# Attention and two MLPs on one core: the subtractions of 1 and the roundings beside the attention go to GpSimd, with a new order

## The chip, the core and the metric

The kernel runs on one core of a Trainium2 chip. The engines of the core work side by side, each through its own queue of instructions in order: TensorE (PE: matmul products, with PEld for its weight loads), VectorE (DVE), ScalarE (ACT), GpSimd (POOL) and SyncE (SP), which here only issues transfers. GpSimd issues some transfers too. The metric is the device time of one execution in microseconds (us), as the median of several runs.

## The reference

Attention over 4 sequences with 8 heads of 576 x 64, in which each row keeps only the scores that lie within tau of its largest, and then two MLPs one after the other over the 2304 tokens.

```python
batch, n_heads, seq, head_dim = (4, 8, 576, 64)        # n_tokens, d_model, d_ff = (2304, 512, 2048)
scores = scale * np.matmul(q, k.transpose(0, 1, 3, 2))
thresh = np.max(scores, axis=-1, keepdims=True) - tau
scores = np.where(scores >= thresh, scores, -1000000000.0)
attn = np.exp(scores - np.max(scores, axis=-1, keepdims=True))
attn = attn / (np.sum(attn, axis=-1, keepdims=True) + 1e-09)
x = np.matmul(attn, v)                                  # to (2304, 512)
h = x @ w_in
g = np.where(h > 0.0, h, 1.0 * (np.exp(np.minimum(h, 0.0)) - 1.0))
x = g @ w_out                                           # first MLP
h = x @ w_in2
out = np.maximum(0.01 * h, h) @ w_out2                  # second MLP
```

The weights come as 64-bit floats; the kernel reads their two 32-bit halves.

## The kernel before, in words

The d_ff dimension is cut into 16 slices f of 128. The work has four stages on TensorE:

1. Attention, and beside it the first MLP's slices f = 0 to 7 for seven blocks of 256 tokens (0 to 1791), whose partial y goes to the scratch tensor `yp`.
2. The same slices for the last 512 tokens, in 512 columns.
3. The first MLP's slices f = 8 to 15 for all tokens, in blocks of 512, added to `yp`.
4. The second MLP, all slices.

**Products in three passes.** An fp32 product is made of three faster ones: each operand is split into a rounded high part and the rest (x into `xh` and `xl`, g into `gh` and `gl`, a weight into `wih` or `woh` and a low part that is named `wil`, `wol` or plain `w` with a number). Every h or y step of one f is 12 products, 4 k or m of 3 passes. Only the first block of 256 tokens runs with whole fp32 operands (`whole` in the code: `h<-x,w` and `y<-gh,w` with 4 products in a step).

**Attention.** A pair of heads with 4 or 5 units of 64 rows is a group's piece; there are 32 pieces. Per unit: scores `s` on TensorE; `ss` on VectorE (scaled, with the row's extreme); threshold `thr`; two steps on ScalarE (`ss`, then the exponential `e` with its sum); the reciprocal `su` on VectorE; `e` times it on GpSimd. Then e is transposed: the first four pieces on TensorE (`y<-ident,e`, then copies into `p`), the other 28 in 32x32 squares on VectorE (`t<-e`) and by 16 copies of 32 partitions from `t` to `p`, issued by SP and by GpSimd. Then `v<-p,v` on TensorE and a copy into `x`.

**One f step beside the attention.** TensorE writes h for slice f into one half of a PSUM bank (`hbank`, two halves in turn). ScalarE takes the exponential into `g`, one of VectorE and GpSimd subtracts 1 (`km`), VectorE takes the min and max with h, which frees the half, one engine rounds g to `gh` (`kg`), VectorE or GpSimd makes `gl = g - gh` (`kgl`), and two steps later TensorE uses both for y. When a block is done, two copies bring y from PSUM to the staging tile `ysa`, and a transfer takes that to `yp`.

**What sets the order.** The program is a list of operations, each with the engines that may do it (the letters in `KN`: A, D, P), a cost and a due time worked out from numbers in `KN`. `Order.run` lays them out greedily on the engines by these costs, and the instructions are written in that order. On the chip every engine then goes through its own list in order and waits where data is not ready.

**End of the attention.** `close_attn` gives the attention's tiles back and opens the tiles of the later stages in their place. It stands behind `end_a`, which before depends on every operation listed so far. `ysa` lies in the pool `ac`, which is given back there.

## Time and profile before

| | us |
|---|---|
| median of 3 runs (lowest, highest) | 1043.79 (1040.55, 1047.26) |
| the profiled execution | 1044.41 |
| its span in the profile | 1042.6 |
| PE busy in the span | 1005.2 (96%) |
| DVE busy | 569.2 (55%) |
| ACT busy | 507.0 (49%) |
| POOL busy | 392.0 (38%) |

The span is the time from the first to the last instruction; the profiled execution took 1.81 us more than that. "Busy" is the time in which at least one instruction ran on the engine. The stages are very unlike each other, so that the shares of the whole span say little about any one of them; the mean granted clock of TensorE over the span is 0.992 of full speed.

### The profile page before, as it was taken

To read this page: it belongs to the slowest core of one execution; us is meant where nothing else is said; L and a number is where in the kernel's file an instruction comes from. 1 tells how busy PE (TensorE), PEld (TensorE's weight loads), DVE (VectorE), ACT (ScalarE), POOL (GpSimd) and SP (SyncE) were. 2 spreads that over 40 slices of the span, in tenths; PEclk is the share of its full clock that TensorE was granted. 3 is DMA by queue.
4 is the path that set the end of the run, shared out by engine and by line. 5 is a ranking of instruction groups with operands and counts; after the bars stand their busy time and mean duration, and the time that the engine had idled before them with its cause. 6 is when DMAs were issued, how large, how long until landed. Compare 5 with 4: busy or idle time off the path is not lost.

```text
span 1042.6 us, 17014 instructions
## 1 busy us (share of the span) xinstructions
PE 1005.2 (96%) x6228; PEld 795.3 (76%) x6228; DVE 569.2 (55%) x1146; ACT 507.0 (49%) x1009; POOL 392.0 (38%) x542
## 2 busy tenths in 40 slices
PE   6869999999999998999999999999999999999998
PEld 3446676677676776888888889888888888888898
DVE  6888778787887856767786457442211311311121
ACT  6967767677777753555455235432222311322221
POOL 5678977567577752444443013440000000000000
PEclk8999999999999999999999999999999999999999
DMA  6676876766778653353443103320100100000010
GB/s 213 209 216 175 221 195 192 227 188 196 201 209 240 192 150 119 102 182 101 143 141 101 61 21 86 118 61 0 41 1 1 41 1 1 22 19 1 1 41 21
DMA packets 47554, 115.93 MB, mean 111 GB/s; under 512 B 9776, under 2 KB 14384, under 8 KB 47472
## 3 DMA queue, kind: packets, MB, share of 16 engines
q1 hardware_dynamic: 42960, 104.36, 33.4%
q0 software_dynamic: 4512, 10.50, 3.7%
q8 instruction: 49, 0.80, 0.3%
q14 instruction: 33, 0.27, 0.1%
HBM read 67.63 MB, written 9.44 MB: 74 GB/s over the span
## 4 chain that ended last, share of the span: by engine, by line
PE 90%; DVE 3%; DMA 2%; ACT 2%; issue 1%; POOL 0%; SPq 0%; ACTq 0%; DVEq 0%; POOLq 0%
PE y L678 37%; PE h L624 22%; PE hb L624 15%; PE v L582 7%; PE s L475 7%; PE y L674 1%; DMA p<-t 1%; PE h L621 1%; DVE w L346 1%; DMA taut<-in_tau_dram 1%; DVE ss L479 1%; DMA wraw<-in_w1i_dram 1%; PE y L513 0%; DVE xl L307 0%; ACT e L493 0%
## 5 line engine op out<-in xcount | busy, mean ns | idle before, releaser
L307 DVE TENSOR_TENSOR gl<-g,gh 128x512 fp32r<-128x512 f32 (+1 forms) x150 | 101.1, 675 | 284.4 <-ACT g L656 265.0
L678 PE MATMUL y<-gh,woh 128*128 128x512 f32 (+1 forms) x704 | 245.5, 349 | 2.1 <-ACT ysa L318 1.4
L678 PE MATMUL y<-gl,woh 128*128 128x512 f32 (+1 forms) x704 | 242.8, 345 | 0.0
L624 PE MATMUL h<-xh,wih 128*128 128x256 f32 (+1 forms) x448 | 153.1, 342 | 9.2 <-ACT g L639 5.1
L678 PEld LDWEIGHTS y<-gh,woh 128*128 128x128 f32 x704 | 132.5, 188 | 29.1 <-issue 8.8
L624 PE MATMUL h<-xl,wih 128*128 128x256 f32 (+1 forms) x448 | 148.6, 332 | 0.7 <-DVE xl L307 0.6
L678 PEld LDWEIGHTS y<-gl,woh 128*128 128x128 f32 x704 | 132.7, 188 | 16.1
L498 POOL TENSOR_SCALAR e<-e,su 128x576 f32<-128x576 f32 x144 | 113.9, 801 | 32.2 <-DVE su L496 30.9
L678 PE MATMUL y<-gh,w 128*128 128x256 f32 (+1 forms) x384 | 124.9, 325 | 0.0
L490 ACT ACTIVATE ss<-ss,thr 128x576 f32<-128x576 f32 x144 | 104.6, 767 | 34.5 <-DVE thr L485 34.4
L479 DVE TENSOR_SCALAR_CACHE_REDUCE ss<-s,scl 128x576 f32<-128x576 f32 x144 | 113.8, 798 | 10.9 <-PE s L475 10.7
L678 PE MATMUL y<-gh,wol 128*128 128x512 f32 (+1 forms) x320 | 117.7, 368 | 0.0
L518 DVE STREAM_TRANSPOSE t<-e 128x640 f32<-128x640 f32 x128 | 101.2, 823 | 17.9 <-POOL e L498 12.5
L493 ACT ACTIVATE e<-ss,taun 128x577 f32<-128x577 f32 x144 | 110.5, 768 | 0.3
L624 PEld LDWEIGHTS h<-xh,wih 128*128 128x128 f32 x448 | 84.2, 188 | 33.2 <-issue 8.8
L475 PE MATMUL s<-in 64*64 64x288 f32 x1152 | 91.3, 428 | 7.8 <-DVE ss L479 7.8
L624 PE MATMUL hb<-xh,wih 128*128 128x512 f32 (+1 forms) x256 | 94.6, 369 | 0.0
L624 PE MATMUL hb<-xl,wih 128*128 128x512 f32 (+1 forms) x256 | 94.5, 369 | 0.0
L582 PE MATMUL v<-p,v 128*64 128x320 f32 (+1 forms) x640 | 87.1, 417 | 5.3 <-DVE p L319 2.3
L624 PEld LDWEIGHTS h<-xl,wih 128*128 128x128 f32 x448 | 84.3, 188 | 10.0 <-DVE xl L307 1.8
L624 PE MATMUL h<-xh,w 128*128 128x256 f32 (+1 forms) x288 | 89.3, 310 | 0.0
L654 ACT ACTIVATE gh<-h 128x512 fp32r<-128x512 f32 (+1 forms) x40 | 22.2, 555 | 132.4 <-PE h L624 132.4
(207 smaller groups left out, 1591.4 us busy)
## 6 DMA issues: line engine op xcount, KB each, us to landing
p<-t SPq DMA_DIRECT2D x128, 100.0 KB, 2.8
p<-t SPq DMA_DIRECT2D x144, 80.0 KB, 3.3
v<-in_kqv_dram SPq DMA_DIRECT2D x32, 320.0 KB, 3.8
in<-in_kqv_dram SPq DMA_DIRECT2D x16, 608.0 KB, 4.2
in<-in_kqv_dram SPq DMA_DIRECT2D x16, 544.0 KB, 4.0
wraw<-in_w1i_dram SPq DMA_DIRECT2D x16, 512.0 KB, 4.3
wraw<-in_w1o_dram SPq DMA_DIRECT2D x16, 512.0 KB, 3.6
wraw<-in_w2i_dram SPq DMA_DIRECT2D x16, 512.0 KB, 3.5
```

Of the source, the lines that this page charges most:

```text
L307: return pick(who, D=(dve(n), lambda: nc.vector.tensor_tensor(**args()), PORT), P=(pool_tt(n), lambda: nc.gpsimd.tensor_tensor(**args())))
L346: ob = op((DVE, dve(512), lambda: nc.vector.scalar_tensor_tensor(out=b().bitcast(U32), in0=top(), scalar=0x80000000, in1=b().bitcast(U32), ...
L475: nc.tensor.matmul(s[z]()[64 * h:64 * h + 64, i, 0:HALF], q()[r, at:at + 64], k()[r, h], start=True, stop=True)
L479: om = [op((DVE, dve(S) + 160, lambda z=z: nc.vector.tensor_scalar(out=ss[z]()[:, 0:S].rearrange("p (j c) -> p j c", j=2), in0=s[z]()[:, : ...
L490: o = op((ACT, act(S) + 95, lambda z=z: nc.scalar.activation(out=ss[z]()[:, 0:S], in_=ss[z]()[:, 0:S], func=AF.Prelu, bias=thr()[:, z:z + ...
L493: oe.append(op((ACT, act(S) + 190, lambda z=z: nc.scalar.activation(out=e[z]()[:, 0:S + 1], in_=ss[z]()[:, 0:S + 1], func=AF.Exp, bias=tau ...
L498: on = [op(pick(KN["kn"], P=(pool_ts(S) + 90, lambda z=z: nc.gpsimd.tensor_scalar(out=e[z]()[:, 0:S], in0=e[z]()[:, 0:S], scalar1=su()[:, ...
L518: turned.append(op((DVE, dve(SX) + 70, lambda z=z, cols=cols: nc.vector.transpose(out=blocks(tg).rearrange("p d c q -> p c d q")[:, :, :, ...
L582: nc.tensor.matmul(ps()[64 * h:64 * h + 64, 0:64 * n], v()[:, h, c, :], blocks(pg)[:, 2 * h:2 * h + 2, c], start=(c == 0), stop=(c == 4))
L624: nc.tensor.matmul(hp(), w_()[:, cs], x_()[:, 0:tb], start=(k == 0 and z == 0), stop=(k == KC - 1 and z == 2))
L654: o1 = op((ACT, actp(tb), lambda: nc.scalar.activation(out=gh()[:, cs], in_=hp(), func=AF.Prelu, alpha=0.01)), [o], [hg, gh], vt)
L678: nc.tensor.matmul(ysl(yg, m), w_()[:, cs], g_()[:, 0:tb], start=(first and z == 0 and share == 0), stop=(last and z == 2 and end))
```

## The change: what it does, and the diff

- The subtraction of 1 (`km`) may only be done by GpSimd; before, VectorE or GpSimd. This holds beside the attention and in the later stages of the first MLP.
- The rounding of g to `gh` beside the attention (`kg`) goes from ScalarE to GpSimd. After the attention it stays on ScalarE.
- The low parts of weights that are made after the attention (`ko`) go from GpSimd to VectorE. The second layer's `gl` (`kgl1`) may be made by GpSimd too.
- Of the 16 copies from `t` to `p` GpSimd issues four instead of five (`NG`), SP twelve instead of eleven.
- `ysa` is taken from the pool `const`, which lasts to the end, and `end_a` depends on what was listed before the last block's copies out of y, not on these and their transfer.
- The other numbers of `KN` (due times) are new, so that the order of nearly all instructions changes. `GROUPS`, `FIRST`, `PT` and `whole` are written in another way with the same values; the new third alternative for `kt` is not chosen.

```diff
-NG = 5
+NG = 4
-SPI = 720
+SPI = 700
...
-    pad=18, stay=1957.74, late=1.3, margin=0, look=0.00236881, warm=2, tu=2525.65, lead=19496.6, wv0=975.379,
-    wv1=-2861.01, early=3673.33, boff=26347.2, bdt=5788.03, yoff=6965.78, coff=5895.83, wb=140.292, w2a=-207.297,
+    pad=18, stay=7714.83, late=1.3, margin=0, look=0.00215667, warm=2, tu=2531.97, lead=19496.6, wv0=975.379,
+    wv1=-2667.23, early=3947.77, boff=37932.2, bdt=5788.03, yoff=12797.6, coff=5895.83, wb=-716.662, w2a=-228.739,
...
-    o3=-792.8, o4=-3200.93, o5=4767.88, o6=-24.0285, mo=-2162.59, ka='P', kl='PA', kh='PA', ko='P', kt='D', kx='A',
-    kxl='DP', km='DP', kg='A', kgl='DP', kgl1='D', kd='P', kc='AD', kn='P', kv='AD')
+    o3=-1828.01, o4=-608.895, o5=4748.06, o6=-26.8192, mo=-4085.5, ka='P', kl='PA', kh='PA', ko='D', kt='D', kx='A',
+    kxl='DP', km='P', kg='P', kgl='DP', kgl1='DP', kd='P', kc='AD', kn='P', kv='AD')
...
-    ysx = []
+    ysx = [const.tile([128, KC, TA], F32, name="ysa")]
...
-    ysx.append(ac.tile([128, KC, TA], F32, name="ysa"))
...
     def evac_a(t0, tb, ybank, ysl, last, xc, vt):
+        since[0] = len(od.ops)
         ys = ys_r.new()
...
-    end_a = op((HOST, 0, lambda: close_attn()), list(od.ops), [], 0)
+    end_a = op((HOST, 0, lambda: close_attn()), od.ops[:since[0]], [], 0)
```

How the order changes is shown at three places.

The first is TensorE between the last `v` of the four pieces that TensorE transposes and the first `v` of a piece whose squares are moved by copies. `h<-x,w` and `y<-gh,w` are whole fp32 products of the first block. Before, the rows from just behind the one `v` to the other:

```order
L621 MATMUL h<-x,w_143 128x256
L621 MATMUL h<-x,w_230 128x256
L475 MATMUL s<-in 64x288 x8
L621 MATMUL h<-x,w_230 128x256 x3
L475 MATMUL s<-in 64x288 x12
L621 MATMUL h<-x,w_324 128x256 x4
L674 MATMUL y<-gh,w_196 128x256 x4
L621 MATMUL h<-x,w_439 128x256 x2
L582 MATMUL v<-p_86,v 64x320 x10
```

There are 11 products of h and 4 of y. With the change, the same place, behind one more row of 8 score products:

```order
L625 MATMUL h<-x,w_143 128x256
L625 MATMUL h<-x,w_236 128x256 x4
L477 MATMUL s<-in 64x288 x8
L625 MATMUL h<-x,w_324 128x256 x2
L477 MATMUL s<-in 64x288 x4
L625 MATMUL h<-x,w_324 128x256 x2
L625 MATMUL h<-x,w_435 128x256 x3
L477 MATMUL s<-in 64x288 x8
L625 MATMUL h<-x,w_435 128x256
L678 MATMUL y<-gh,w_179 128x256 x4
L678 MATMUL y<-gh,w_287 128x256 x2
L586 MATMUL v<-p_86,v 64x320 x10
```

There are 13 products of h and 6 of y, and the score products stand in smaller rows between them.

The second place is GpSimd's list in the middle of the attention stage, around the start of the fifth block of 256 tokens. Before (`e` is the multiplication by the reciprocal sum, `g` the subtraction of 1, DMA the issue of copies from `t` to `p`):

```order
L498 TENSOR_SCALAR e_91<-e_91,su 128x576
L568 DMA p_87<-t_89 32x640 x5
L498 TENSOR_SCALAR e_92<-e_92,su 128x576
L498 TENSOR_SCALAR e_93<-e_93,su 128x576
L643 TENSOR_SCALAR g<-g 128x256
L498 TENSOR_SCALAR e_90<-e_90,su 128x576
L498 TENSOR_SCALAR e_91<-e_91,su 128x576
L643 TENSOR_SCALAR g<-g 128x256
L308 TENSOR_TENSOR gl<-g,gh 128x256
L643 TENSOR_SCALAR g<-g 128x256
```

With the change, the list at the same block:

```order
L572 DMA p_87<-t_89 32x640
L572 DMA p_87<-t_89 32x800 x2
L572 DMA p_87<-t_89 32x640
L502 TENSOR_SCALAR e_92<-e_92,su 128x576
L502 TENSOR_SCALAR e_93<-e_93,su 128x576
L647 TENSOR_SCALAR g<-g 128x256 x2
L502 TENSOR_SCALAR e_90<-e_90,su 128x576
L502 TENSOR_SCALAR e_91<-e_91,su 128x576
L314 TENSOR_SCALAR gh<-g 128x256
L311 TENSOR_TENSOR gl<-g,gh 128x256
L647 TENSOR_SCALAR g<-g 128x256
```

Two subtractions stand in a row behind four issues and two steps of `e`, and the rounding `gh` is in the list.

The third place is SP at the end of the attention: the last piece's copies, the last block's transfer to `yp`, and the first loads of raw weights for the later slices. Before:

```order
L568 DMA p_87<-t_89 32x640
L568 DMA p_87<-t_89 32x800 x4
L731 DMA yp_dram<-ysa 512x1x256
L326 DMA wraw<-in_w1i_dram 128x1024
L326 DMA wraw<-in_w1o_dram 128x1024
```

With the change:

```order
L572 DMA p_87<-t_89 32x640
L572 DMA p_87<-t_89 32x800 x2
L329 DMA wraw<-in_w1i_dram 128x1024
L737 DMA yp_dram<-ysa 512x1x256
L329 DMA wraw<-in_w1o_dram 128x1024
```

The first weight load has moved ahead of the transfer to `yp`. On ScalarE the first `xh` of the last 512 tokens still stands behind the last step of the attention stage, in both orders.

## Rows read from the trace of the kernel before

**Rows 1.** Windows by stage: start:end, length, busy us and instructions by engine, clock, DMA share, GB/s.

```profile
0.00:20.00 20.00, 13.10 (x83) 5.72 (x83) 11.86 (x33) 11.31 (x20) 9.97 (x21) 0.83 0.62 221
20.00:55.00 35.00, 28.34 (x257) 16.89 (x259) 29.72 (x70) 32.91 (x65) 24.89 (x32) 0.95 0.67 209
55.00:80.00 25.00, 17.48 (x103) 10.96 (x101) 22.31 (x43) 16.64 (x32) 18.80 (x25) 0.87 0.66 196
...
100.00:385.00 285.00, 276.22 (x2468) 201.23 (x2467) 223.06 (x555) 208.99 (x464) 204.13 (x329) 1.00 0.72 202
385.00:405.00 20.00, 16.52 (x114) 12.46 (x113) 7.66 (x15) 4.39 (x10) 4.63 (x8) 1.00 0.53 153
405.00:700.00 295.00, 294.59 (x1389) 247.42 (x1388) 196.62 (x295) 137.42 (x231) 112.49 (x106) 1.00 0.32 102
```

**Rows 2.** Timeline of PE, 60 to 77 us: start, us, instruction, idle before and releaser.

```profile
64.79 0.72 PE L475 MATMUL s<-in 64*64 64x288 f32 x8 [2.41 <-DVE ss L479]
66.92 1.24 PE L475 MATMUL s<-in 64*64 64x288 f32 x8 [1.42 <-DVE ss L479]
...
70.99 1.89 PE L674 MATMUL y<-gh,w 128*128 128x256 f32 x8
...
76.56 0.95 PE L582 MATMUL v<-p,v 128*64 128x320 f32 x3 [2.20 <-DMA p<-t]
```

**Rows 3.** The chain that ended last, around the end of the attention: start, us, what.

```profile
389.91 5.26 PE y L678 x45
...
397.32 3.58 DMA yp_dram<-ysa
...
401.39 0.64 ACT xh L313
```

**Rows 4.** Timeline of PE, 395 to 403 us.

```profile
395.94 0.39 PE L678 MATMUL y<-gh,woh 128*128 128x256 f32 x1 [0.78 <-DVE ysa L319]
...
396.50 3.12 PE L582 MATMUL v<-p,v 128*64 128x320 f32 x20
402.07 0.50 PE L624 MATMUL h<-xh,wih 128*128 128x512 f32 x1 [2.46 <-ACT xh L313]
402.80 0.50 PE L624 MATMUL h<-xl,wih 128*128 128x512 f32 x1 [0.22 <-DVE xl L307]
```

**Rows 5.** Timeline of PE, inside one group of h products at 382 us.

```profile
382.75 0.38 PE L624 MATMUL h<-xh,wih 128*128 128x256 f32 x1 [0.53 <-ACT g L639]
```

**Rows 6.** DVE by line and shape: count, busy us, mean ns of one, idle before.

```profile
L479 DVE TENSOR_SCALAR_CACHE_REDUCE ss<-s,scl 128x576 f32<-128x576 f32 x144 | 113.8, 798 | 10.9 <-PE s L475 10.7
L518 DVE STREAM_TRANSPOSE t<-e 128x640 f32<-128x640 f32 x128 | 101.2, 823 | 17.9 <-POOL e L498 12.5 <-DMA p<-t 4.8 <-DMA in<-in_kqv_dram 0.2
...
L346 DVE SCALAR_TENSOR_TENSOR w<-wraw,w 128x512 uint32<-128x512 uint32 x64 | 48.0, 750 | 1.2
...
L647 DVE SCALAR_TENSOR_TENSOR g<-g,h 128x256 f32<-128x256 f32 x52 | 21.5, 416 | 14.9 <-PE h L624 9.4 <-ACT g L639 4.1 <-POOL g L643 0.6
...
L641 DVE TENSOR_SCALAR g<-g 128x256 f32<-128x256 f32 x23 | 7.7, 343 | 5.0 <-ACT g L639 4.8
```

**Rows 7.** ACT by line and shape, the rounding and the exponential of g.

```profile
L313 ACT ACTIVATE gh<-g 128x256 fp32r<-128x256 f32 x56 | 23.0, 411 | 22.5 <-DVE g L647 15.4 <-PE y L678 6.9
L639 ACT ACTIVATE g<-h 128x256 f32<-128x256 f32 x60 | 22.7, 379 | 33.0 <-PE h L624 23.7 <-PE h L621 3.6 <-DVE g L647 1.9
```

**Rows 8.** POOL by line and shape.

```profile
L498 POOL TENSOR_SCALAR e<-e,su 128x576 f32<-128x576 f32 x144 | 113.9, 801 | 32.2 <-DVE su L496 30.9
L568 POOL DMA_DIRECT2D p<-t x140 | 70.5, 508 | 23.1 <-DVE t L518 9.5 <-PE s L475 5.4 <-DVE ss L479 3.0
...
L308 POOL TENSOR_TENSOR wol<-w,woh 128x512 fp32r<-128x512 f32 x16 | 21.3, 1331 | 16.0 <-ACT woh L313 15.7
```

**Rows 9.** Line L643: ns of one as min/median/max, first and last start.

```profile
L643 POOL TENSOR_SCALAR g<-g x44: 394/404/840, 59.9 to 580.8; 128x256 f32<-128x256 f32 x41, 128x512 f32<-128x512 f32 x3
```

**Rows 10.** Line L568, SP's issue of copies.

```profile
L568 SPq DMA_DIRECT2D p<-t x308: 507/589/1911, 64.0 to 391.9; - x154
```

More of the change, by code (lines that the diff above doesn't have):

```diff
@@ L30 @@
 NU = S // 64
-GROUPS = [(b, u0, u1) for b in range(B) for u0, u1 in ((0, 4), (4, NU))]
+CUTS = (4,)
+GROUPS = [(b, u0, u1) for b in range(B) for u0, u1 in zip((0, *(CUTS if b == 0 else (4,))), (*(CUTS if b == 0 else (4,)), NU))]
+HEADS = [(0, 256)]
+FIRST = HEADS + [(t, TA) for t in range(256, 1792, TA)]
 UM = 5
 WT = 32 * UM
-BESIDE = 7
 GP = 1
-PT = ()
-NG = 5
+PT = set()
+NG = 4
+LP = 0
 POOLI = 520
-SPI = 720
+SPI = 700
 PM = ()
@@ L689, in attn_moe_kernel, with block @@
     ypdone = {}
-    def block(layer, t0, fs, tb, deps, hps, yrings, evac, vt0, dt, reg=False):
-        if reg and t0 < NATIVE * TA:
+    since = [0]
+    def block(layer, t0, fs, tb, deps, hps, yrings, evac, vt0, dt, reg=False, whole=False):
+        if whole:
             xc = [(None, x[:, k, t0:t0 + tb], deps[k]) for k in range(KC)]
@@ L762, in attn_moe_kernel @@
     kept, ready = None, {}
+    PT.update(order[len(order) - LP:])
     for gi, p in order:
@@ L787, in x_deps @@
                  if b * S + 64 * u0 < t0 + tb and b * S + 64 * u1 > t0] for k in range(KC)]
-    for i in range(BESIDE):
-        need = next(n for t, n in ends if t >= (i + 1) * TA)
-        block(0, i * TA, list(range(FH)), TA, x_deps(i * TA, TA), h_a, ya, evac_a,
-              need * TU + KN["boff"] + (KN["b0"], KN["b1"], KN["b2"], 0)[min(i, 3)], KN["bd0"] if i == 0 else KN["bdt"],
-              reg=True)
+    for i, (t0, tb) in enumerate(FIRST):
+        need = next(n for t, n in ends if t >= t0 + tb)
+        block(0, t0, list(range(FH)), tb, x_deps(t0, tb), h_a, ya, evac_a,
+              need * TU + KN["boff"] + (KN["b0"], KN["b1"], KN["b2"], 0)[min(i, 3)],
+              KN["bd0"] if i < NATIVE else KN["bdt"], reg=True, whole=i < NATIVE)
         if i == NATIVE - 1:
@@ L814, in dt @@
         return 24 * mm(tb)
-    rest = [(t0, tb) for t0, tb in ((t, min(TB, NT - t)) for t in range(BESIDE * TA, NT, TB))]
+    rest = [(t0, tb) for t0, tb in ((t, min(TB, NT - t)) for t in range(sum(FIRST[-1]), NT, TB))]
     ysb = {}
```

16 lines of the change are left out of this document (9 added, 7 removed).

## The prediction

> **What bounds the kernel now.** I first read busy time by stage, since the shares of the whole span mix stages with different limits. PE is busy for 1005.2 of 1042.6 us, and the change leaves every product of PE as it is, so what can move is the 37.4 us in which PE stands still, and the clock. The windows say where these lie [rows 1]: 6.9 us up to 20 us, 6.7 up to 55, 7.5 from 55 to 80, 8.8 in the 285 us of the attention stage proper (100 to 385), 3.5 at its end (385 to 405) and 0.4 from 405 to 700. The rest is the tail behind the last product, whose instructions keep their engines and order. The granted clock is below full speed only up to 80 us, where it mixes the levels 1.2 and 2.4 GHz (means 0.83, 0.95, 0.87).
>
> Then I asked for each of these stretches what PE waited for. Up to 55 us ScalarE is busy for 32.91 of 35 us in the second window and VectorE for 29.72 [rows 1]: the two prepare both the attention's first pieces and the first 16 weights, and PE gets its work late whatever its order. From 55 to 80 us PE waits 2.41 and 1.42 us for VectorE's score step and 2.20 us for the copies of the first piece that VectorE transposes [rows 2]; these three are 6.0 of the 7.5 us. At the end of the attention a chain shows: the transfer of `ysa` to `yp` lands, and only then does ScalarE make the first `xh` of the next stage, in memory that the attention gave back [rows 3]; PE waits 0.78, 2.46 and 0.22 us there [rows 4]. In the attention stage proper the idle time is made of short stalls such as the one shown [rows 5]: between two products of one group of h PE waits about 0.5 us for an engine that reads the previous h in the other half of the same bank.
>
> **The change, part by part.**
>
> *First pieces, 55 to 80 us.* VectorE's list between the score step of the 21st unit and the last transposition of the piece it closes loses two steps on weights, one score step and one copy: 2 x 0.750 + 0.798 = 2.3 us, the copy left out [rows 6]. SP has one copy more to issue for that piece, 0.589 us [rows 10], so that the piece is due 1.7 us earlier. PE has 19 products of the first block in that stretch instead of 15 (the first two pieces of order above), and four at 1.89 / 4 = 0.47 us [rows 2] (each product is recorded twice, so that x8 is four of them) fill 1.9 us more. At best that is 3.6 us. It is not sure to be had: the waits of 2.41 and 1.42 us are for VectorE, whose whole list up to the 32nd score step stays within about 1 us of the length it had. I take 2.5 us, between 1.7 and 3.6; the ends are 0 and 7.5.
>
> *End of the attention.* `ysa` no longer lies in what is given back, so that `xh` need not wait for the transfer (3.58 us). What is late next is PE's own last product, whose operands `gh` and `gl` do lie there: `xh` starts behind it and takes 0.64 us [rows 3]. Then `xl` is in GpSimd's list with the change, where a subtraction of 512 columns takes 1.33 us [rows 8], against 0.7 on VectorE. PE's idle time becomes 0.78 (the last products of y still wait for the first copy out of their tile), 0.74 for `xh` with a signal, and some 1.1 until `xl`: 2.6 instead of 3.46 us. The gain is 0.9 us, with ends at 0 and 3.5.
>
> *Subtractions and roundings beside the attention.* 23 subtractions of 256 columns leave VectorE (0.343 us each, 7.9 in all [rows 6]) and 48 roundings leave ScalarE (0.411 us, 19.7 [rows 7]); the roundings are of the same form on GpSimd as the subtraction, whose median there is 0.404 [rows 9]. GpSimd gains 23 + 48 at 0.404 = 28.7 us and loses 28 issues at 0.508 = 14.2 [rows 8]; with five more `gl` it stands at some 220 of 285 us instead of 204 [rows 1]. None of the three engines bounds the stage, before or after; PE does, with 276 of 285 us. So the 27 us taken from VectorE and ScalarE are worth nothing by themselves, and they cost nothing where GpSimd answers in time. Two counts in PE's order bear on that. Inside the groups of h (without each block's first) 18 products wait for an engine in the order before, and 18 with the change: the short stalls stay, 8.8 us in all. And between a group of h and the second one after it, which needs the same half of the bank, PE now has as little as about 3.0 us of other work: for example 12 products of h, 3 of y and 8 score products, 15 x 0.117 [rows 3] and two to three times 0.72 / 2 us at the clock of full speed [rows 2]. Six places lie between 3.0 and 3.6 us, against one before. The half is free after exponential, subtraction and min/max: 0.379 + 0.404 + 0.416 = 1.2 us [rows 6, 7, 9], 1.3 with signals, which leaves 1.7 us for queues. I take nothing for them; the other end is the second rival's price.
>
> *Copies.* SP issues 12 x 0.589 = 7.1 us per piece instead of 6.5 [rows 10]. Of the 28 pieces one made PE wait, the one of 2.20 us [rows 2], so beyond it 0.6 us more is hidden by PE's products. At the last piece PE has 135 products and a `v` between score and `v`, before 123: 1.4 us more cover.
>
> *After the attention.* The 37 subtractions of 512 columns that go to GpSimd and the 48 low parts of weights that go to VectorE are beside 294.59 us of 295 in which PE does not stop [rows 1]. A step of h and y there is 24 products of 512 columns, and the half of h has three such half-steps (8 us) until it is needed. Nothing, with ends of 0 and a few us.
>
> The sum, against the profiled execution: 1044.41 - 2.5 - 0.9 = **1041 us**. That execution is 0.6 us above the median of the three runs, which lie 6.7 us apart; I leave the sum there.
>
> **The rivals.**
>
> *Nothing comes of it: 1044 us.* The first piece's wait only turns into waits for score steps, and `xl` on GpSimd eats what the transfer gave. For it speaks that VectorE and ScalarE are full up to 55 us [rows 1] and that the new chain at the end is 2.6 us even when it goes well.
>
> *GpSimd holds the bank: 1056 us, slower.* Its list puts subtractions behind four issues and two steps of `e` (second piece of order). Those are 4 x 0.508 + 2 x 0.801 = 3.6 us [rows 8], and an issue waits for all transpositions of its piece. Where that row stands ahead of the subtraction at one of the six narrow places, the half comes free 3.6 - 1.7 = 1.9 us late, 11.6 us for six; the six of the 18 waits inside groups that are for VectorE's min/max would grow by some 0.5 us, 3 more. The point from which it decides is 1.7 us of GpSimd work ahead of the subtraction. For it speaks that every subtraction now has this one queue; against it, that the order was laid out with GpSimd's rows in it and that GpSimd is free a fifth of the time. Contention is part of this rival: the longest subtraction on GpSimd took 0.840 us against a median of 0.404 [rows 9]. The Trainium skill, "SBUF — State Buffer", section "Who interferes with whom", says that a VectorE instruction with two SBUF inputs and a GpSimd instruction that reads SBUF exclude each other, and that the later one stands until the first is done; the trace agrees so far as that 0.44 us goes. By that rule alone, with the 0.44 us at twelve places and no spare left, the sum would be 1046 us.
>
> *Most of the waits go: 1027 us, faster.* All idle time from 55 to 80 us (7.5), the low clock there (13% of 17.48 busy us, 2.3), all 3.5 us at the end of the attention and half of the short stalls (4.4) are 17.7 us [rows 1]. Against it: the 18 waits inside groups are still there, and the chain of `xh` has its own length.
>
> **How the numbers follow.** Something between 1036 and 1046, forecast and first rival together, holds most of the chance: 0.5 for the forecast, 0.3 for nothing. The slow rival has 0.1, of which some is a part of its price that stays within 1%; the fast one 0.1, likewise. About 1% (10 us) is what a measurement of this kernel can tell from no change. Faster by more than that: 0.08; slower: 0.08; within: 0.84. The range must leave out no more than 2 in 10: from 1033, half-way into the fast rival and just at 1%, to 1050, where four of the six narrow places lose their 1.9 us.
>
> **What would show it.** In the profile after: PE's first wait for `v<-p,v` of a moved piece (2.20 us before) is gone or below 1 us, and PE busy from 55 to 80 us is 19 to 21 us. At the end of the attention `xh` waits for PE, not for the transfer, and PE's idle time from the last y to the second product of h is 2 to 3 us. From 100 us to the last piece PE's idle time is 8 to 10 us. GpSimd's busy time there is some 77% of the stretch. Wrong would be: waits of PE's h for VectorE's or GpSimd's g of over 1 us each in the attention stage, or an idle PE between 405 and 700 us, where a raw weight that lands late could now hold GpSimd's next subtraction behind it.

## The result

The changed kernel takes 1054.83 us (median of 4 runs, 1053.97 to 1055.67) against 1043.09 of the kernel before: a ratio of 1.011, 95% interval 1.008 to 1.014. It is slower by 11.7 us where a gain of 3.4 us against the profiled execution was forecast, and the time lies outside the range of 1033 to 1050. The profiled execution took 1054.27 us with a span of 1052.3, 9.7 us more than before.

The windows by stage of the kernel after (start:end, length, busy us and instructions of PE, PEld, DVE, ACT and POOL, clock, DMA share, GB/s) answer to [rows 1]:

```profile
55.00:80.00 25.00, 18.15 (x118) 10.84 (x119) 22.38 (x47) 18.19 (x36) 16.19 (x25) 0.93 0.71 211
...
100.00:385.00 285.00, 270.69 (x2416) 192.71 (x2412) 230.24 (x537) 194.88 (x417) 216.52 (x362) 1.00 0.74 204
```

PE is idle for 14.3 us from 100 to 385 instead of 8.8; from 55 to 80 us it is busy for 18.15, little more than the 17.48 of before. The end of the attention has moved from the window 385 to 405 into the next one, so fixed times no longer compare the same work. PE's list helps: it has 1601 steps in both kernels, and behind its 60th, 120th, 250th, 560th and 600th step PE has done the same set of steps. Cut at the ends of those steps, the windows of the kernel before are these:

```profile
0.00:84.50 84.50, 63.42 (x472) 36.22 (x472) 66.86 (x152) 63.92 (x123) 57.09 (x82) 0.90 0.65 204
84.50:126.00 41.50, 40.83 (x306) 25.92 (x306) 33.06 (x81) 30.34 (x64) 37.86 (x51) 1.00 0.76 203
126.00:205.60 79.60, 76.87 (x701) 56.20 (x700) 61.83 (x156) 57.47 (x127) 57.60 (x94) 1.00 0.75 212
205.60:389.90 184.30, 178.93 (x1622) 132.06 (x1621) 142.42 (x355) 134.86 (x302) 125.83 (x208) 1.00 0.70 196
389.90:418.90 29.00, 25.52 (x139) 20.55 (x138) 17.57 (x27) 10.42 (x19) 7.40 (x7) 1.00 0.41 120
```

and those of the kernel after:

```profile
0.00:84.40 84.40, 63.28 (x469) 34.13 (x469) 63.80 (x145) 62.88 (x120) 51.59 (x79) 0.90 0.61 198
84.40:130.60 46.20, 42.62 (x308) 26.33 (x305) 36.43 (x85) 28.95 (x63) 41.00 (x58) 1.00 0.68 184
130.60:211.40 80.80, 77.12 (x700) 56.53 (x701) 66.55 (x153) 55.30 (x119) 62.34 (x108) 1.00 0.71 204
211.40:399.70 188.30, 180.54 (x1621) 132.08 (x1621) 146.30 (x345) 122.03 (x263) 134.16 (x233) 1.00 0.74 202
399.70:428.80 29.10, 26.68 (x139) 21.17 (x138) 16.22 (x23) 9.39 (x16) 8.46 (x12) 0.94 0.25 75
```

Read the second column downwards: the first 60 steps take the same time, steps 61 to 120 (the rest of the first block) 4.7 us more, the next 130 steps 1.2, steps 251 to 560 4.0, the end of the attention 0.1 more, and what follows 0.2 less. So the 9.7 us lie in the attention, beside the blocks. In its three windows PE's idle time (length less busy) is 15.0 us instead of 8.8; the other 3.7 us of the 9.9 there are longer records of products.

The startup shows why nothing came of the first pieces. PE's timeline of the kernel after, 55 to 81 us (start, us, instruction, idle before and releaser), answers to [rows 2]:

```profile
67.08 0.72 PE L477 MATMUL s<-in 64*64 64x288 f32 x8 [1.66 <-DVE ss L481]
69.63 0.67 PE L625 MATMUL h<-x,w 128*128 128x256 f32 x2 [1.83 <-DVE gh L651]
70.81 0.99 PE L625 MATMUL h<-x,w 128*128 128x256 f32 x2 [0.52 <-DVE gh L651]
```

The wait of 2.20 us for the copies is gone, as forecast, and 1.66, 1.83 and 0.52 us for VectorE stand where 2.41 and 1.42 us for it stood in [rows 2]. At the end of the attention, PE's timeline answers to [rows 4]:

```profile
408.78 0.39 PE L682 MATMUL y<-gh,woh 128*128 128x256 f32 x1 [0.78 <-DVE ysa L322]
...
410.17 0.49 PE L628 MATMUL h<-xh,wih 128*128 128x512 f32 x1 [0.77 <-ACT xh L316]
411.52 0.50 PE L628 MATMUL h<-xl,wih 128*128 128x512 f32 x1 [0.86 <-POOL xl L311]
...
413.09 0.63 PE L628 MATMUL h<-xh,wih 128*128 128x512 f32 x1
```

`xh` waits there for PE's last product of y, as the row of ScalarE says, and no longer for the transfer of [rows 3]:

```profile
409.49 2.19 ACT L316 ACTIVATE xh<-x 128x512 fp32r<-128x512 f32 x4 [10.78 <-PE y L682]
```

The idle time is 0.78 + 0.77 + 0.86 = 2.4 us, where 2.6 were forecast and 3.46 stood before. But the products behind it take 0.63 us in place of 0.39 to 0.40, and the window there (columns as above) says why:

```profile
412.00:415.50 3.50, 3.50 (x11) 2.71 (x10) 2.99 (x5) 0.33 (x1) 0.55 (x1) 0.56 0.77 246
```

Behind the three pauses (clock 1.00 from 408 to 412) the granted clock is 0.56 in the mean over 3.5 us, most of it at the level of 1.2 GHz, which costs 1.5 us (44% of 3.5). Before, the pauses of 0.78, 2.46 and 0.22 us were followed by no such fall: the windows from 400 to 410 us have 1.00. That takes the gain of the shorter wait away.

### The profile page after: what moved, and what is told of

Same layout as the page of the kernel before. It is cut to its first block, busy times and chain, and to the rows that moved or that the text cites. A ratio compares the mean times of both kernels' runs of the same rounds, so it can differ in the third digit from the quotient of the medians.

```text
span 1052.3 us, 17038 instructions
## 1 busy us (share of the span) xinstructions
PE 1009.8 (96%) x6228; PEld 794.7 (76%) x6228; DVE 577.7 (55%) x1129; ACT 485.1 (46%) x951; POOL 376.3 (36%) x589
## 4 chain that ended last, share of the span: by engine, by line
PE 84%; DVE 5%; DMA 2%; POOL 2%; ACT 1%; issue 1%; SPq 1%; DVEq 0%; ACTq 0%; POOLq 0%
PE y L682 36%; PE h L628 21%; PE hb L628 15%; PE v L586 5%; PE s L477 5%; DVE t L522 2%; DMA p<-t 2%; PE h L625 1%; DVE ss L481 1%; POOL e L502 1%; SPq L572 1%; DMA in<-in_kqv_dram 1%; DVE thr L489 0%; POOL w L311 0%; PE y L678 0%
## 5 line engine op out<-in xcount | busy, mean ns | idle before, releaser
L310 DVE TENSOR_TENSOR gl<-g,gh 128x512 fp32r<-128x512 f32 (+1 forms) x141 | 94.4, 669 | 278.4 <-ACT g L660 259.8
L682 PEld LDWEIGHTS y<-gh,woh 128*128 128x128 f32 x704 | 132.5, 188 | 32.6 <-issue 10.7
L311 POOL TENSOR_TENSOR gl<-g,gh 128x256 fp32r<-128x256 f32 (+1 forms) x35 | 27.9, 799 | 304.9 <-ACT g L660 218.6
L502 POOL TENSOR_SCALAR e<-e,su 128x576 f32<-128x576 f32 x144 | 111.0, 781 | 22.1 <-DVE su L500 18.8
L647 POOL TENSOR_SCALAR g<-g 128x256 f32<-128x256 f32 (+1 forms) x104 | 54.0, 520 | 154.8 <-ACT g L643 150.4
L628 PEld LDWEIGHTS h<-xl,wih 128*128 128x128 f32 x448 | 84.5, 189 | 11.0 <-POOL xl L311 2.5
```

The costliest lines, as they stand in the source:

```text
L310: return pick(who, D=(dve(n), lambda: nc.vector.tensor_tensor(**args()), PORT), P=(pool_tt(n), lambda: nc.gpsimd.tensor_tensor(**args())))
L311: P=(pool_tt(n), lambda: nc.gpsimd.tensor_tensor(**args())))
L502: on = [op(pick(KN["kn"], P=(pool_ts(S) + 90, lambda z=z: nc.gpsimd.tensor_scalar(out=e[z]()[:, 0:S], in0=e[z]()[:, 0:S], scalar1=su()[:, ...
L628: nc.tensor.matmul(hp(), w_()[:, cs], x_()[:, 0:tb], start=(k == 0 and z == 0), stop=(k == KC - 1 and z == 2))
L647: P=(pool_ts(tb), lambda: nc.gpsimd.tensor_scalar(out=g()[:, cs], in0=g()[:, cs], scalar1=-1.0, scalar2=1.0, op0=ALU.add, op1=ALU.mult))),
L682: nc.tensor.matmul(ysl(yg, m), w_()[:, cs], g_()[:, 0:tb], start=(first and z == 0 and share == 0), stop=(last and z == 2 and end))
```

## The experiments

The first theory was my second rival's: GpSimd's queue holds the bank of h (**theory GpSimd's queue**). The rival to it: the loss is in the new order of the lists, whichever engine does the steps (**theory order**). Times are medians; ratios are to the kernel before on the same chip, with 95% intervals.

**a_order_old_engines.** The planner plans as in the kernel after; only what is emitted differs.

```diff
-P=(pool_ts(tb), lambda: nc.gpsimd.tensor_scalar(...))
+P=(pool_ts(tb), lambda: (nc.vector.tensor_scalar(...) if reg else nc.gpsimd.tensor_scalar(...)))
-o1 = op(hi_of(KN["kg"] if reg else "A", tb, ...), [o], [g, gh], vt)
+o1 = op([(*a[:2], lambda: nc.scalar.mul(out=gh()[:, cs], ...), *a[3:]) for a in hi_of(...)], [o], [g, gh], vt)
```

> The kernel after, with the order of every engine kept as it is planned: only the 56 subtractions of the 256-wide blocks beside the attention are carried out by VectorE and the 48 roundings by ScalarE instead of GpSimd. PE's list and SP's list are the same row for row. Theory GpSimd's queue (the subtractions and roundings wait behind copies and steps of e, the bank of h comes free late): the 10 us lost between 90 and 345 us come back, 1043 to 1047 us. Theory order (the lost time lies in how PE's products, and so the dependences between engines, now stand, whichever engine does the step): 1053 to 1057 us, since VectorE and ScalarE have room but PE's order is unchanged.

Measured: 1055.62 us, ratio 1.0118 (1.0100 to 1.0135). Nothing comes back: the theory of GpSimd's queue falls for these steps.

**b_order_new_engines.** The mirror of it in the kernel before.

```diff
-D=(dve2(tb), lambda: nc.vector.tensor_scalar(...), PORT)
+D=(dve2(tb), lambda: (nc.gpsimd.tensor_scalar(...) if reg else nc.vector.tensor_scalar(...)), PORT)
+# and the rounding of reg blocks emitted by nc.gpsimd.tensor_scalar
```

> The kernel before, with the order kept as it was planned: only 15 subtractions of 256 columns go from VectorE to GpSimd and 48 roundings from ScalarE to GpSimd, so that all of them beside the attention are GpSimd's, as in the kernel after. Theory GpSimd's queue: slower than before by some 10 us, 1050 to 1056 us. Theory order: within 3 us of the kernel before, 1041 to 1046 us.

Measured: 1045.55 us, 1.0020 (1.0004 to 1.0035). The subtractions and roundings cost some 2 us (0.2%) in an order that did not expect them on GpSimd.

**b_ysa_const.** The new place of `ysa` alone.

```diff
-    ysx = []
+    ysx = [const.tile([128, KC, TA], F32, name="ysa")]
...
-    ysx.append(ac.tile([128, KC, TA], F32, name="ysa"))
...
-    end_a = op((HOST, 0, lambda: close_attn()), list(od.ops), [], 0)
+    end_a = op((HOST, 0, lambda: close_attn()), od.ops[:since[0]], [], 0)
```

> The kernel before with one part of the change alone: the staging tile ysa lies in memory that outlives the attention, and the attention's memory is given back without waiting for the last copies and the transfer out of ysa. PE's order is the same row for row. Either theory of the lost time: 0 to 2 us faster than before, 1041 to 1043 us, since the wait of 2.46 us at the end of the attention falls to about 1.5 us. If it is slower than before, the place of the tile itself costs something.

Measured: 1041.40 us, 0.9974 (0.9962 to 0.9986), the fastest kernel of this study, faster than both. Its window of PE's steps 561 to 600:

```profile
388.10:415.10 27.00, 25.14 (x139) 20.79 (x138) 15.71 (x27) 10.46 (x19) 4.92 (x5) 1.00 0.41 125
```

27.0 us instead of 29.0, at full clock: with `xl` on VectorE and the pauses at 0.78, 0.72 and 0.35 us the clock stays up. The rest of the 4.2 us between the two profiles lies ahead of PE's 60th step, which comes at 81.7 us here and at 84.5 before. In the profiles of five kernels with the sequence of before up to there it comes at 81.7 to 84.8 us, so 3 us at the start tell nothing.

**a_numbers_old_letters.** The kernel after, its engine choices set back and planned anew.

```diff
-ko='D', ... km='P', kg='P', kgl='DP', kgl1='DP'      # threshold: D=(270, ...)
+ko='P', ... km='DP', kg='A', kgl='DP', kgl1='D'      # threshold: D=(150, ...)
```

> The kernel after with the engine choices of before (subtractions on VectorE or GpSimd, roundings on ScalarE, low parts of late weights on GpSimd, the cost of the threshold step as before), planned anew with the new due numbers, four of sixteen copies and the new place of ysa. Theory GpSimd's queue: near the kernel before, 1041 to 1047 us. Theory order (the new due numbers lay the attention stage out worse): 1050 to 1058 us.

Measured: 1063.88 us, 1.0196 (1.0181 to 1.0211). It goes beyond what either theory said: with the new due numbers, another set of engines gives a still worse plan. (The change also raises the planner's cost of the threshold step on VectorE from 150 to 270; this kernel has the old one.)

Next I asked whether PE's own list carries the loss. Four kernels gave the planner PE's list as fixed and let it lay the other lists around it:

```diff
+        want = iter(PE_ORDER)
+        turn = [next(want)]
...
         def push(o):
+            if o.alts[0][0] == PE and o.seq != turn[0]:
+                return
```

> The kernel after with its own due numbers, engine choices, copies and place of ysa, but with PE's list of the kernel before: the planner may give PE nothing but the next step of that list, and lays the other engines' lists around it by its own numbers. Theory PE order (the 10 us lie in the sequence in which PE takes its products): the time falls to that of the kernel before or to that with the new place of ysa, 1040 to 1046 us. Theory helpers (the lists of VectorE, ScalarE, GpSimd and the DMA queues cost it, as the due numbers lay them): 1051 to 1057 us.

Measured: 1064.36 us, 1.0177 (1.0154 to 1.0201).

> The kernel before with its own due numbers, engine choices and copies, but with PE's list of the kernel after. Theory PE order: 1050 to 1058 us. Theory helpers: 1042 to 1047 us.

Measured: 1064.94 us, 1.0185 (1.0161 to 1.0210).

> The kernel after with the first 120 steps of PE's list (to the end of the first block, some 126 us) as in the kernel before and the other 1481 as in the kernel after; the other lists are laid around it. Theory PE order: the part of the loss that lies before some 130 us, 4 us by the records, comes back, so 1049 to 1052 us. Theory helpers: 1053 to 1057 us.

Measured: 1066.62 us, 1.0196 (1.0167 to 1.0225).

> The kernel after with the first 120 steps of PE's list as in the kernel after and the rest as in the kernel before. Theory PE order: the part of the loss behind some 130 us, 6 us by the records, comes back, so 1046 to 1050 us. Theory helpers: 1053 to 1057 us.

Measured: 1062.27 us, 1.0156 (1.0130 to 1.0182).

All four are slower than both kernels, which neither theory had: PE's list of one kernel and helper lists laid by the other's numbers make a third kernel, worse than either. Which list is to blame is not a question that can be asked of one list alone.

From here on nothing is planned: a kernel carries the sequence of all 4482 steps with the engine of each, and emits it.

```diff
+        for e, i in LIST:
+            next(alt for alt in self.ops[i].alts if alt[0] == e)[2]()
+        return 0
```

**order_b_engines_a, order_a_engines_b.** The sequence of one kernel (before: with the new place of `ysa`) with all engines of the other.

> All that the change does except its order: code, engine choices, copies, place of ysa and late engine choices of the kernel after, with all lists emitted in the sequence of the kernel before with the new place of ysa (no planning). 389 of 4481 steps run on another engine than there. Theory order (the 10 us lie in how the lists of all engines stand to each other, and not in which engine does a step): 1041 to 1046 us. Theory engines (the choices together cost it, copies and late choices included): 1050 us or more.

Measured: 1063.19 us, 1.0168 (1.0143 to 1.0194).

> The reverse: code, engine choices and copies of the kernel before with the new place of ysa, with all lists emitted in the sequence of the kernel after. Theory order: 1051 to 1057 us. Theory engines: 1041 to 1046 us.

Measured: 1061.78 us, 1.0159 (1.0133 to 1.0184). Both are slower than both parents. They also exchange choices that the planner makes freely between two engines by their load, so they do not yet say which choice costs it.

**a_repair, a_guard.** Two tries at the short waits between two groups of h, which share a bank. a_repair moves products in the sequence; a_guard tells the planner:

```diff
 # a_repair, the first place (PE's list)
-MATMUL h<-x,w_648 128x256 x3
 MATMUL s<-in 64x288 x8
-MATMUL h<-x,w_648 128x256
 MATMUL y<-gh,w_487 128x256
+MATMUL h<-x,w_648 128x256 x4
 # a_guard
-    h_a = Ring(lambda: (lambda i: hbank[:, i])(next(halves)), 2)
+    h_a = Ring(lambda: (lambda i: hbank[:, i])(next(halves)), 1)
```

> The kernel after with the sequence of all lists kept, except that 88 products of h in 30 groups are emitted later: behind the min/max of the group before them (which reads the other half of the same bank) and one further step of PE. 16 places where that is not possible stay. Theory bank (the order after has more places where PE steps into a group of h while the other half is still read, and waits some 0.55 us at each): PE's idle time in the attention stage falls by 3 to 5 us and the time to 1049 to 1052 us. Theory spread (the loss has many causes, and moving h takes the fit of the other lists away): 1054 to 1060 us.

Measured: 1059.56 us, 1.0143 (1.0118 to 1.0168).

> The kernel after with one number changed, the count of the ring of h halves from 2 to 1, and planned anew: the planner now knows that a group of h has to wait for the reads of the group before it, since both halves lie in one bank. 75 of 79 groups then begin behind these reads (33 in the kernel after). Theory bank: the short waits of some 0.5 us inside groups of h go, and the time falls by 3 to 8 us, 1047 to 1052 us. Theory fit (due numbers and planner's model are made for each other, any new plan loses): 1058 to 1068 us, with other waits in place of these.

Measured: 1067.58 us, 1.0229 (1.0200 to 1.0258). In a_guard PE no longer waits for ScalarE's `g` at all (20 to 425 us), but 10.7 us for VectorE's score step, where the kernel after waits 1.7, and 5.0 us for the copies, where it waits 0.6. In a_repair its waits for ScalarE's `g` fall from 2.9 to 1.5 us and those for VectorE's rise from 4.0 to 5.3, with 4.9 in the whole products instead of 3.1. Moving h costs more than the short waits do.

**b_all_choices_of_after, a_all_choices_of_before.** Now only what the change chooses on purpose is exchanged: subtractions, roundings, late low parts, and the copies (by their number of the sixteen). Free choices stay.

```diff
 # engines in LIST, here for b_all_choices_of_after; sequence as before
-copies 3, 6, 9, 12, 15 of sixteen on GpSimd; g - 1 on VectorE or GpSimd; gh on ScalarE; late low parts on GpSimd
+copies 3, 7, 11, 15 of sixteen on GpSimd; g - 1 on GpSimd; gh on GpSimd; late low parts on VectorE
```

> The sequence of the kernel before (with the new place of ysa) in all lists, and every engine choice that the change makes on purpose: all subtractions and roundings beside the attention on GpSimd, the 37 late subtractions too, 84 copies moved to SP and 56 to GpSimd (four of sixteen), the 48 late low parts on VectorE. Choices that the planner makes freely stay as before. Theory places (the choices cost next to nothing, the loss lies at places of the new order): 1041 to 1046 us. Theory choices (an order that doesn't expect the copies on SP waits for them): 1050 us or more.

Measured: 1051.84 us, 1.0079 (1.0054 to 1.0103): 1.05% above b_ysa_const.

> The reverse: the sequence of the kernel after in all lists, with every one of those choices set back to that of the kernel before (five of sixteen copies on GpSimd in their old places). Theory places: 1053 to 1057 us. Theory choices: 1046 us or less.

Measured: 1060.25 us, 1.0157 (1.0132 to 1.0181). Neither theory holds as put: the choices cost it in the order of before, and setting them back costs it in the order after. With two runs from above this makes four corners (ratios to the kernel before; the two sequences also differ in the choices that the planner makes freely):

| | choices of before | choices of the change |
|---|---|---|
| sequence of before, new place of `ysa` | 0.9974 | 1.0079 |
| sequence of after | 1.0157 | 1.011 |

The new sequence costs 1.8% with the old choices and 0.3%, which the intervals do not tell from nothing, with the new ones; the choices cost 1.05% in the old sequence and give back 0.5% in the new one. The two do not add up, so the loss of the change cannot be shared out between them.

**b_copies_only, b_all_but_copies.** The choices split in two, in the sequence of before: the first item of that diff, and the other three.

> The kernel before with the new place of ysa, its sequence in all lists, and of the engine choices only the copies changed: four of sixteen on GpSimd, at other numbers of the sixteen, so that 84 go from GpSimd to SP and 56 from SP to GpSimd; PE's, VectorE's and ScalarE's lists stay row for row. All choices together were 10 us above the kernel with the new place of ysa. Theory copies (they are most of these 10 us: twelve issues in SP's list make a piece late, and hold the loads behind them): 1048 to 1052 us. Theory sum of choices (GpSimd's subtractions and roundings, or the late choices, cost it): 1041 to 1045 us.

Measured: 1054.59 us, 1.0092 (1.0071 to 1.0113).

> The complement: the kernel before with the new place of ysa, its sequence, and all deliberate choices of the change but the copies (subtractions, roundings, late subtractions on GpSimd, late low parts on VectorE); PE's and SP's lists stay row for row. Theory copies: 1041 to 1044 us (1041.4 and up to 1.5 for the subtractions and roundings). Theory sum of choices: 1047 to 1051 us.

Measured: 1042.35 us, 0.9984 (0.9971 to 0.9997). This is the cleanest cut of the study. Everything but the copies leaves the kernel faster than before and within 0.1% of b_ysa_const; the copies alone cost 1.0092 - 0.9974 = 1.18%, 12 us, on top of b_ysa_const, and 1.0079 - 0.9984 = 0.95%, 10 us, when they come on top of the other choices (b_all_choices_of_after against b_all_but_copies). What is exchanged is number and place together: the sequence was planned for five copies on GpSimd, and the 56 that come to it stand where SP had them.

Of this, 3.9 us lie in PE's steps 61 to 120, 3.0 in steps 121 to 250 and 3.8 in steps 251 to 560. The windows of steps 61 to 120, first of b_ysa_const:

```profile
81.70:123.20 41.50, 40.83 (x305) 26.36 (x306) 33.13 (x81) 30.29 (x64) 38.18 (x52) 1.00 0.79 206
```

then of b_copies_only:

```profile
82.90:128.30 45.40, 43.23 (x306) 26.96 (x306) 41.51 (x80) 28.87 (x62) 36.23 (x49) 0.96 0.66 184
```

PE's, VectorE's and ScalarE's lists are the same, yet VectorE is busy for 41.51 us instead of 33.13 with one instruction less. Some of its steps have become longer. One of them, with GpSimd's row of work beside it (timeline of b_copies_only, 113 to 119 us):

```profile
113.69 1.28 POOL L317 TENSOR_TENSOR w<-w,wih 128x512 fp32r<-128x512 f32 x1
114.02 3.63 DVE L495 TENSOR_SCALAR thr<-nm,taup 128x2 f32<-128x2 f32 x1
114.93 1.46 POOL L508 TENSOR_SCALAR e<-e,su 128x576 f32<-128x576 f32 x2
116.37 1.25 POOL L317 TENSOR_TENSOR w<-w,woh 128x512 fp32r<-128x512 f32 x1
117.69 1.44 ACT L500 ACTIVATE ss<-ss,thr 128x576 f32<-128x576 f32 x2 [4.62 <-DVE thr L495]
```

The threshold step has two numbers per partition, and takes 3.63 us. It begins while GpSimd is at `w`, stands through two steps of `e` and another `w`, each of which starts as the one before ends, and is over at 117.65, when the last of them ends (117.62). ScalarE waits 4.62 us for it. PE hardly does: it is busy for 4.26 of 4.50 us there, but the granted clock is 0.62, part of the time at the level of 1.2 GHz, behind pauses of 0.53, 0.48 and 0.49 us at 110 to 113 us for `gh` of VectorE, `xh` of ScalarE and `xl` of GpSimd:

```profile
113.00:117.50 4.50, 4.26 (x24) 2.82 (x24) 4.38 (x5) 0.07 (x1) 4.47 (x6) 0.62 0.73 187
```

The next long one does reach PE. It ends at 128.74, 0.03 us after another unbroken row of GpSimd; ScalarE, 2.04 us late by it, comes to the exponential of `g` at 130.88, and PE has its longest wait of the stage:

```profile
125.24 3.50 DVE L495 TENSOR_SCALAR thr<-nm,taup 128x2 f32<-128x2 f32 x1
131.29 0.38 PE L630 MATMUL h<-xh,wih 128*128 128x256 f32 x1 [2.32 <-ACT g L645]
```

GpSimd's row is not new. At the same place b_ysa_const has the same `w`, two `e` and `w` (109.41 to 113.47 us), and the same threshold step comes 2.0 us after the row's start instead of 0.33 and takes 0.26 us:

```profile
110.75 1.47 POOL L498 TENSOR_SCALAR e<-e,su 128x576 f32<-128x576 f32 x2
111.41 0.26 DVE L485 TENSOR_SCALAR thr<-nm,taup 128x2 f32<-128x2 f32 x1
```

So the moved issues change when the step meets the row. They do make GpSimd wait longer for VectorE's last transposition (`p` for `t`, 85 to 410 us; total, times, longest), first in b_ysa_const, then in b_copies_only, then in the kernel after:

```profile
POOL p L568 <- DVE t L518: 9.5, 10, 1.7
POOL p L578 <- DVE t L528: 21.4, 16, 2.7
POOL p L572 <- DVE t L522: 8.1, 9, 1.4
```

That the longer waits bring step and row together is not shown. And the kernel after, whose order was planned for four copies, does not have them (3.5 us more stand there as waits of these issues that the profile puts down to no engine). So the price of 10 to 12 us is that of copies in places that were not planned for them, and this mechanism is not seen in the kernel after.

**splice_b_then_a, splice_a_then_b.** Sequence and engines of one kernel up to PE's 120th step, those of the other from there. Of the 654 steps of all lists that either sequence has placed by then, 647 are the same.

```diff
-LIST = after
+LIST = before[:k] + [s for s in after if s not in before[:k]]   # k: PE's 120th step
```

> Sequence and engines of the kernel before with the new place of ysa up to PE's 120th step (the end of the first block, where PE has done the same steps in both orders), from there those of the kernel after. Theory places (each part of the order keeps its own loss): the kernel after lost 7.4 us against the kernel with the new place of ysa up to that step, so 1054.8 - 7.4 = 1047 us, 1045 to 1050. Theory fit (the parts live from how far the other lists have come, and lose when they are put together): 1053 us or more.

Measured: 1047.81 us, 1.0050 (1.0029 to 1.0070).

> The reverse splice: the kernel after up to PE's 120th step, from there sequence and engines of the kernel before with the new place of ysa. Theory places: 1041.4 + 7.4 = 1049 us, 1046 to 1051. Theory fit: 1053 us or more.

Measured: 1051.22 us, 1.0068 (1.0047 to 1.0088). The first is within 1 us of what the theory of places said, the second 0.2 us above the end of its range, and both are below the 1053 us of the other. That is partly luck: 2.7 of the 7.4 us lie ahead of PE's 60th step, where profiles scatter by 3 us, and the two losses against b_ysa_const, 0.76% and 0.94%, add up to 1.7% where the kernel after has 1.36%. Their windows of steps 61 to 120, first splice_b_then_a:

```profile
84.80:126.20 41.40, 40.73 (x303) 25.64 (x303) 32.97 (x81) 30.22 (x63) 37.90 (x51) 1.00 0.76 200
```

then splice_a_then_b:

```profile
85.30:132.90 47.60, 43.10 (x307) 25.42 (x304) 37.80 (x86) 29.16 (x64) 40.47 (x56) 0.98 0.68 184
```

Each part of a sequence brings its own time along, 41.4 us from the order before and 47.6 from the order after. So the order's loss sits at places, and a large part of it, 5 to 6 us, in the rest of the first block (46.20 - 41.50 us in the two kernels, 47.60 - 41.40 in the splices).

No single wait fills these places. In the kernel after, PE's waits in steps 61 to 120 are of 0.15 to 1.10 us, 3.5 us in all instead of 0.7, for VectorE, ScalarE and GpSimd in turn, the longest of them this one:

```profile
128.57 0.39 PE L628 MATMUL h<-xl,wih 128*128 128x256 f32 x1 [1.10 <-POOL xl L311]
```

And the same whole products of h come in eight rows between other work instead of four, and are recorded as busy for longer, first before and then after (busy us, mean ns, idle before):

```profile
L621 PE MATMUL h<-x,w 128*128 128x256 f32 x32 | 7.7, 382 | 0.0
L625 PE MATMUL h<-x,w 128*128 128x256 f32 x32 | 8.8, 398 | 1.3 <-DVE gh L651 0.7 <-ACT g L643 0.5
```

The held threshold steps of b_copies_only are not there: VectorE's eight steps of 128x2 take 2.7 us in both kernels in this stretch.

## Why the prediction was wrong

The step that failed is the attention stage, which the sum put at nothing: "the short stalls stay, 8.8 us in all". From PE's 60th to its 560th step it takes 9.9 us more, with 15.0 us of idle PE instead of 8.8 and 3.7 us of longer records of products. Two things that the prediction took to cost nothing stand behind that term, the copies and the new order, and the runs show that neither is free.

**The copies: not hidden.** It said of them: "beyond it 0.6 us more is hidden by PE's products", and 1.4 us of cover at the last piece. I weighed twelve issues on SP against PE's cover and counted 28 issues that leave GpSimd; in fact 84 leave it and 56 come to it. GpSimd's list has steps of every softmax and block behind an issue. In the sequence of before the copies alone cost 10 to 12 us, in places that were not planned for them. The kernel after, planned for four, is 0.3% above b_all_choices_of_after, so the new order does not win this back; and setting the choices back within it (a_all_choices_of_before) costs 0.5% more. How much of the loss of the kernel after is due to the copies stays open. SP's longer rows are not free either: one load for the scores, issued behind twelve copies, lets PE wait 1.47 us, the only such wait in the attention stage of either kernel.

```profile
234.98 10.13 SPq L572 DMA_DIRECT2D p<-t  x12
245.21 0.53 SPq L438 DMA_DIRECT2D in<-in_kqv_dram  x1
250.98 1.20 PE L477 MATMUL s<-in 64*64 64x288 f32 x16 [1.47 <-DMA in<-in_kqv_dram]
```

**The new order itself: no term.** The sum had terms for steps that change their engine and none for the due numbers, which move nearly everything. Two counts from the lists stood for that (18 waits inside groups of h before and after, six narrow bank places). The waits of PE for readers of h did stay (88 to 420 us: 10 for `g` of ScalarE and 3 for VectorE's before, 6 and 5 after, one of these 1.5 us, which is the prediction's own sign of being wrong). The rest of the loss came at places of other kinds, which a count of one kind cannot see. The largest totals in PE's waits of the kernel after besides ScalarE's `g`, 88 to 420 us (total, times, longest; the second has 0.9 us of the end of the attention):

```profile
PE h L628 <- DVE g L651: 4.0, 5, 1.5
...
PE h L628 <- POOL xl L311: 2.0, 2, 1.1
```

The longest of the first, 1.53 us at 143.24, comes behind a held threshold step. The timeline of the kernel after at 136 to 141 us:

```profile
137.74 1.46 POOL L502 TENSOR_SCALAR e<-e,su 128x576 f32<-128x576 f32 x2
...
138.11 2.56 DVE L489 TENSOR_SCALAR thr<-nm,taup 128x2 f32<-128x2 f32 x1
139.18 0.39 POOL L314 TENSOR_SCALAR gh<-g 128x256 fp32r<-128x256 f32 x1
139.55 0.40 POOL L647 TENSOR_SCALAR g<-g 128x256 f32<-128x256 f32 x1
139.92 0.72 POOL L311 TENSOR_TENSOR gl<-g,gh 128x256 fp32r<-128x256 f32 x1
```

It begins while GpSimd is at `e` and ends at 140.67; GpSimd's run ends at 140.64. Behind it VectorE has two transpositions and a score step ahead of the min/max that PE waits for. It is no more than one place: with the subtractions and roundings taken out of that run (a_order_old_engines) the time stays. And ScalarE's wait for the threshold, which grows from 34.4 us in the whole profile before, does not set the time. It is as long in b_all_but_copies, which is within 0.1% of b_ysa_const, as in the kernel after; here first the kernel after:

```profile
ACT ss L494 <- DVE thr L489: 50.0, 42, 4.3
ACT ss L500 <- DVE thr L495: 50.5, 39, 3.0
```

**Subtractions and roundings: nothing, right.** Between the two sides they are worth +0.2% in the order of before and -0.1%, within the noise, in the order after. The rival "GpSimd holds the bank" named 1056 us, close to what was measured, and is wrong as a mechanism: VectorE's min/max waited for GpSimd's subtraction for 5.4 us in five waits (85 to 410 us; 0.6 before), but the time did not come back when these steps went elsewhere. That the number was near is luck. A GpSimd subtraction has a median of 408 ns where [rows 9] has 404.

Its remark on contention pointed the right way with the wrong victim and size. I priced 0.44 us on GpSimd's step; in the kernel after it was a VectorE step that took up to 2.56 us.

**First pieces: 2.5 us, not had.** The wait for the copies went, as said; I had named the risk (VectorE's list up to there keeps its length), and it came: PE is busy for 18.15 us from 55 to 80 us, where 19 to 21 were forecast, and its first 60 steps end at 84.4 us instead of 84.5. Profiles scatter by 3 us there, so the second number alone could not have told 2.5 us.

**End of the attention: mechanism right, size lost to the clock.** `xh` waits for PE, idle 2.4 us (forecast 2.6); the term of 0.9 us is lost to 1.5 us of low clock. Alone, on the order of before, the same part of the change gains 0.26%, 2.7 us, and 2.0 us in its own window, which is more than the term: `xl` stays on VectorE there, PE waits 0.35 us for it instead of 0.86, and the clock stays up.

**After the attention: nothing, right.** From PE's 600th step to the end 623.7 us before and 623.5 after. (A small sum of the range is off: four narrow places at 1.9 us end at 1049 us, not at 1050.)

**What stays open.** Whether four copies of sixteen on GpSimd have an order as good as the one before for five, and how the loss of the order after divides between the due numbers and the copies that it was planned with: kernels planned with another mix of numbers, engines or PE lists are all 0.5% or more above it, so planning anew could not separate them. Exchanging engines in a fixed sequence does not separate them either, since it puts steps in places that were planned for others.

## What to carry to other kernels

Where a planner lays out all queues, a new set of due numbers is a change of its own and the largest one in the diff: cut both profiles at points where the bottleneck engine has done the same set of steps, and compare stage by stage before explaining anything by the edits. To test an edit apart from its plan, keep the sequence of all queues and exchange only the engine; planning again, or fixing one queue and planning the rest, tests a third kernel. Do it in both sequences: here the same choices cost 1.05% in one and gave back 0.5% in the other. Look for the mechanism of a test kernel in the kernel that is to be explained, too. And before a waiting instruction is put into a busy queue, ask not how long it takes there but what will pile up behind it.

## What the runs showed of the hardware

A VectorE step can stand through several GpSimd instructions that follow each other without a gap. The threshold step at its shortest, its median and its longest, in ns: before, and in b_copies_only (in the kernel after the longest is 2565):

```profile
L485 DVE TENSOR_SCALAR thr<-nm,taup x80: 166/228/735, 10.4 to 379.8; 128x2 f32<-128x2 f32 x64, 128x1 f32<-128x1 f32 x16
```

```profile
L495 DVE TENSOR_SCALAR thr<-nm,taup x80: 166/228/3631, 10.5 to 389.5; 128x2 f32<-128x2 f32 x64, 128x1 f32<-128x1 f32 x16
```

At 114.02 and 125.24 us in b_copies_only and at 138.11 us in the kernel after it ended 0.03 us after the last of four or five such instructions, of which the longest took 1.28 us. Most held steps end sooner. This one of the kernel after is over 0.02 us after the first of two steps of `e`, while the second follows without a gap:

```profile
148.84 1.47 POOL L502 TENSOR_SCALAR e<-e,su 128x576 f32<-128x576 f32 x2
149.01 0.60 DVE L489 TENSOR_SCALAR thr<-nm,taup 128x2 f32<-128x2 f32 x1
```

Of the 17 threshold steps of the kernel after that take over 0.40 us behind its 80th us, 3 stand through more than one instruction (2, 3 and 5). What decides between the two is open. The Trainium skill, "SBUF — State Buffer", section "Who interferes with whom", lists `tensor_scalar` among the VectorE operations that can take the port pair shared with GpSimd, and says that whoever issues first has it for the whole instruction while the other is blocked. That one engine stands while the other works agrees, and so does the wait of one instruction in most places; the waits through two to five are longer than the page leads one to expect.

The clock does not follow the idle time alone. A pause of 2.46 us before the 512-wide products left it at 1.00, and so did three of 0.78, 0.72 and 0.35 us in b_ysa_const. Three pauses of 0.78, 0.77 and 0.86 us within 3.5 us in the kernel after were followed by 1.2 GHz for some 3.4 us, and three of 0.53, 0.48 and 0.49 us within 3.3 us in b_copies_only by a mean of 0.62 over 4.5 us. In the profile of splice_b_then_a, whose execution took 1054.69 us against a median of 1047.81, one of 3.23 us for a late load was followed by 0.57 over 8 us. PE's row and the window there:

```profile
249.15 1.24 PE L483 MATMUL s<-in 64*64 64x288 f32 x8 [3.23 <-DMA in<-in_kqv_dram]
```

```profile
247.50:255.50 8.00, 6.35 (x37) 5.10 (x38) 2.41 (x7) 1.41 (x3) 1.76 (x3) 0.57 0.56 123
```
